# A fused attention and MLP kernel: a table moves engine orders, squares and copies change engine, pairs of transfers become one

## The chip, the cores and the metric

The kernel runs on one core of one Trainium2 chip. The metric is the device time of one execution in microseconds (us), the median of several runs. TensorE is called PE, VectorE DVE, ScalarE ACT, GpSimd POOL and SyncE SP. Transfers are issued from SP, POOL and ACT and are carried out by the core's 16 DMA engines.

## The reference

Cosine attention over 8 batches, 12 heads, 448 tokens and a head size of 64, followed by an MLP over the 3584 tokens whose activation is h·cos(h):

```python
q_n = q / (np.linalg.norm(q, axis=-1, keepdims=True) + 1e-06)
k_n = k / (np.linalg.norm(k, axis=-1, keepdims=True) + 1e-06)
scores = np.matmul(q_n, k_n.transpose(0, 1, 3, 2)) / tau
attn = softmax(scores)                      # tau = 0.1
x = (attn @ v).transpose(0, 2, 1, 3).reshape(3584, 768)
h = x @ w_in                                # 768 x 2048
out = (h * np.cos(h)) @ w_out               # 2048 x 768
```

## The kernel before

**Tiles and stages.** A *quad* is four heads of one batch: three quads to a batch, 24 in all. For each quad q and k are loaded (`Qf`, `Kf`, 448 KB each), squared (`square`), summed over the head size (`add`, DVE), turned into inverse norms (`inverse`: Ln and Exp on ACT, an addition and a reciprocal on DVE), scaled (`scale`) and transposed: by PE and a copy for the first quads (`transpose`), by a transposing DMA later (`turn`). `scores` makes seven pairs of score banks in PSUM, each evacuated by one Exp on ACT into a tile `E` (L556). `attend` multiplies by v.

The softmax's row sums come in two ways. For quads 0 to 5 PE multiplies `E` by ones (`spread`) and ACT inverts the 128-partition result. For quads 6 to 23, in rounds of two quads, `sums` makes a few rows of sums with `sel`, and `invert` takes their Ln and Exp, writes 8 rows of 448 numbers to a scratch tensor `rscr` in DRAM (issued from ACT, L648), and reads them back spread over 64 partitions each into `R` (two buffers; issued from SP, L654, two transfers for each quad, one for each half of the partitions). POOL then multiplies `AVs` by `R` into the MLP's input `xT` (L657).

The MLP works batch by batch: `m1` (96 matmuls of 128x448 a batch, L675, in 8 pairs of PSUM banks; ACT and DVE make h·cos(h) from each pair, L688 to L694), then `m2` over row tiles of 128 tokens (28 tiles, two halves of 384 columns, 16 matmuls each, L703). DVE copies each half to `osb` (three buffers, L711), and SP stores the tile in two transfers of 64 rows (L717).

**What sets the order.** Every operation is recorded by `op` in a `Planner`, which has a duration for each and lays them out per engine. PE's order is the order of recording. Ahead of the first MLP stage the planner is `strict`: ACT, DVE and POOL keep their recorded order as well (`behind`, L50). After that, whichever ready operation has the earliest due time goes first. `VISITS` and `LATER` say, batch by batch, after how many `m2` matmuls PE takes up pieces of the attention of later batches. Waits between engines are put in from the recorded reads and writes. SP, POOL and ACT each issue their transfers in their order, so one that waits holds up those behind it.

**Transfers.** A transfer is described by an access pattern for each side: a list of [step, count] pairs, the outermost first. A store of 64 rows (before) has the patterns [[5376, 64], [1, 768]] in DRAM and [[768, 64], [1, 768]] in SBUF, and a read of `R` has [[0, 64], [1, 896]] and [[896, 64], [1, 896]].

Other lines that are named later: L797 are matmuls without use that keep PE running in the first stretch (`warm`), L399 the loads of q and k, L411 those of v, L421 and L426 those of the two weight matrices (`W1`, `W2`), L524 the copies behind PE's transposes.

Of the kernel before, what the change touches and what calls it, by code (L numbers as in the profile page):

```python
# [9 lines left out]
ALU = mybir.AluOpType  # L10
# [6 lines left out]
class Op:  # L17
    __slots__ = ("i", "eng", "dur", "fn", "reads", "writes", "deps", "dma", "lat", "start", "end",
                 "count", "waits", "known", "prio", "moves", "mode", "chain", "behind", "lead", "packet", "lock")


class Planner:
# [20 lines left out]
    def op(self, eng, dur, fn, r=(), w=(), after=(), dma=None, moves=0, mode="f", chain=None, keep=False, lead=0.0,  # L43
           packet=74, lock=False):
        o = Op()
        o.i, o.eng, o.dur, o.fn, o.dma, o.moves, o.mode, o.chain = (
            len(self.ops), eng, dur, fn, dma, moves, mode, chain)
        o.lat = self.FIRST + moves + self.LAST if dma else self.LAT[eng]
        o.behind, o.lead, o.packet, o.lock = None, lead, packet, lock
        if keep or self.strict and eng in ("act", "dve", "pool"):  # L50
            o.behind, self.tail[eng] = self.tail.get(eng), o
        o.reads, o.writes = tuple(r), tuple(w)
        deps = {a.i for a in after if a is not None}
        for x in o.reads:
            if x in self.last_write:
                deps.add(self.last_write[x].i)
        for x in o.writes:
            if x in self.last_write:
                deps.add(self.last_write[x].i)
            deps.update(p.i for p in self.readers.get(x, ()))  # L60
        deps.discard(o.i)
        o.deps = sorted(deps)
        for x in o.reads:
            self.readers.setdefault(x, []).append(o)
        for x in o.writes:
            self.last_write[x] = o
            self.readers[x] = []
        self.ops.append(o)
        return o
# [12 lines left out]
    PASSES, SPREAD = 0, 1.5  # L82

    def plan(self):

        rng = random.Random(1)
        shift = [0.0] * len(self.ops)
        least = max(o.end for o in self.pass_(shift))
        for _ in range(self.PASSES):
            n = rng.choice((8, 30, 100))  # L90
            i = rng.randrange(len(shift) - n)
            tried = list(shift)
            for k in range(i, i + n):
                tried[k] += rng.gauss(0.0, self.SPREAD)
            end = max(o.end for o in self.pass_(tried))
            if end <= least:
                least, shift = end, tried
        self.order = self.pass_(shift)
        return self.order

    def pass_(self, shift):
# [12 lines left out]
        for o in ops:  # L114
            if o.eng == "pe":
                urge[o.i] = t
                t += o.dur
        later = None
        behind = {}
        for o in reversed(ops):  # L120
            if o.eng == "pe":
                if later is not None:
                    urge[o.i] = min(urge[o.i], urge[later.i] - o.dur)
                later = o
# [10 lines left out]
        pe = [o.i for o in ops if o.eng == "pe"]  # L135
# [139 lines left out]
def bass_cosine_attention__then__act_gcu_kernel(  # L275
# [43 lines left out]
    n2 = ring("n2", 2, [128, 4 * NJ], F32)  # L319
    nrm = ring("nrm", 2, [128, 4 * NJ], F32)  # L320
    rr = ring("rr", 2, [128, 4 * NJ], F32)
    ne = ring("ne", 2, [128, 4 * NJ, 2], F32)
# [39 lines left out]
    for i in range(2):  # L362
        op("dve", 0.1, lambda e, i=i: e.memset(ne[i].ap()[:, :, 1], 1e-6), w=[("eps", i)])
# [67 lines left out]
    def jr(t, w, part, off=0):  # L431
        return bass.AP(t, off + w * H + part[0], [[2 * H, 128], [NJ, 2], [1, part[1] - part[0]]])

    def square(qd, w, eng, part=ALL[0], after=()):
        s, u = qd % 3, qd % 2
        j0, j1 = part
        n = (j1 - j0) / NJ
        f, sq, nm = ((Qf, sqq, "Q"), (Kf, sqk, "K"))[w]
        src = f[s].ap()[:, :, j0:j1]
        dst = sq.ap().rearrange("p (r j) d -> p r j d", r=2)[:, :, j0:j1]  # L440
        if part == ALL[0]:
            src, dst = src.rearrange("p r j d -> p (r j) d"), sq.ap()
        if eng == "act":
            op("act", 0.1 + 0.83 * n, lambda e: e.activation(dst, src, ACT.Square), r=cut(nm + "f", s, part),
               w=cut("sq" + nm, 0, part))
        else:
            op(eng, (1.68 if eng == "pool" else 1.05) * n, lambda e: e.tensor_tensor(dst, src, src, ALU.mult),  # L447
               r=cut(nm + "f", s, part), w=cut("sq" + nm, 0, part), after=after, lock=True)

        def add():  # L450
            return op("dve", 0.07 + 0.95 * n, lambda e: e.tensor_reduce(  # L451
                out=n2[u].ap()[:, H * w:H * w + H] if part == ALL[0] else jr(n2[u], w, part),
                in_=dst, axis=AX.X, op=ALU.add),
                r=cut("sq" + nm, 0, part), w=cut("n2%d" % w, u, part))

        return add

    def inverse(qd, w0, w1, part=ALL[0], after=()):
# [5 lines left out]
        if part == ALL[0]:  # L464
            n = slice(H * w0, H * w1)
            t, z, o = n2[u].ap()[:, n], nrm[u].ap()[:, n], rr[u].ap()[:, n]
        else:
            t, z, o = (jr(a[u], w0, part) for a in (n2, nrm, rr))
# [11 lines left out]
        two_ = ne[u].ap()[:, H * w0:H * w1]  # L480
# [7 lines left out]

    def scale(qd, w, eng="pool", part=ALL[0]):
# [3 lines left out]
        rb = bass.AP(rr[u], w * H + j0, [[2 * H, 128], [NJ, 2], [1, j1 - j0], [0, D]])  # L493
# [16 lines left out]
    def transpose(qd, which, bk, part=ALL[0]):  # L510
# [12 lines left out]
        dst = t[u].ap()[:, j0:j1].rearrange("p j a x -> p (j a x)")  # L523
        op("dve", 0.07 + 0.067 * (j1 - j0), lambda e: e.tensor_copy(dst, src), r=whole(bk),  # L524
# [113 lines left out]
    def invert(quads, bk):  # L638
# [9 lines left out]
        op("act", 0.3, lambda e: e.dma_start(rscr.ap()[8 * n:8 * n + rows, :], Zs[z].ap()[0:32 * np_:16, :]),  # L648
           r=[("Zs", z)], w=[("rs", n)], dma=("rs", z), moves=0.05, lead=LEAD)
        for i, qd in enumerate(quads):  # L650
            u, sl, b = qd % 2, qd % NA, qd // QB
            for r in range(2):
                ap = bass.AP(rscr, (8 * n + 4 * i + 2 * r) * S, [[0, 64], [S, 2], [1, S]])
                op("sp", 0.6, lambda e, r=r, u=u, ap=ap: e.dma_start(R[u].ap()[64 * r:64 * r + 64], ap),  # L654
                   r=[("rs", n)], w=[("R", u, r)], dma=("R", u, r), moves=0.85, packet=140, lead=LEAD)
# [3 lines left out]
                r=[("AV", sl), ("R", u, 0), ("R", u, 1)], w=[("x", b % 2, qd % QB)], lead=LEAD, lock=True)  # L659
# [37 lines left out]
    def m2(t, h, f0, f1, bk):  # L697
# [11 lines left out]
        if f1 == NNB:  # L709
            so = t % 3  # L710
            op("dve", 0.475, lambda e: e.tensor_copy(osb[so].ap()[:, HW * h:HW * h + HW], bank(bk, HW)),  # L711
               r=whole(bk), w=[("o", so, h)])
            if h:
                for sg in range(2):
                    b, cc = divmod(128 * t + 64 * sg, S)
                    dst = bass.AP(out.tensor, (S * b + cc // 64) * KM, [[NJ * KM, 64], [1, KM]])
                    op("sp", 0.6, lambda e, sg=sg, dst=dst: e.dma_start(dst, osb[so].ap()[64 * sg:64 * sg + 64, :]),  # L717
                       r=[("o", so, 0), ("o", so, 1)], w=[("out", t, sg)], dma=("store", so, sg), moves=0.55, packet=121)
# [15 lines left out]
    LATER = {19: 3, 10: -1, 18: -2, 5: 3, 4: 1, 17: 4, 7: -1, 21: -2, 22: -1, 15: -2, 9: 1}  # L734
# [100 lines left out]
    adds[0]()  # L835
# [5 lines left out]
    adds[1]()  # L841
# [19 lines left out]
    addk = square(2, 1, "act")  # L861
# [86 lines left out]
    for c in range(B):  # L948
# [106 lines left out]
```

## Time and profile before

| | |
|---|---|
| median of 3 runs | 425.83 us (425.01 to 428.05) |
| the profiled execution | 424.88 us, of it 423.0 us from the first to the last instruction |
| PE, ACT, DVE, POOL busy | 406.1, 306.3, 269.5, 200.9 us |
| granted PE clock | 1.00 throughout |
| bytes moved | 62.94 MB: 53.87 MB read from HBM, 11.14 MB written |

The batches' `m1` stages begin on PE at 34.4, 89.0, about 148, 195.6, 245.8, 292.9, 346.0 and 379.7 us. The profile's columns are: for a window the span, then each engine's busy time (with its instructions in brackets), the granted clock, the mean busy share of the 16 DMA engines and the GB/s that they moved. In the chain of waits each row has its start, its length and the work that it stands for. In the DMA view a queue's row has its packets, its MB, and the packets' time as a share of 16 engines' span. A row of the issues has the transfer, the queue it is issued from, its count, the size of one, and the median time to landing.

### The profile page before, as it was taken

To read this page: it belongs to the slowest core of one execution; us is meant where nothing else is said; L and a number is where in the kernel's file an instruction comes from. 1 tells how busy PE (TensorE), PEld (TensorE's weight loads), DVE (VectorE), ACT (ScalarE), POOL (GpSimd) and SP (SyncE) were. 2 spreads that over 40 slices of the span, in tenths; PEclk is the share of its full clock that TensorE was granted. 3 is DMA by queue.
4 is the path that set the end of the run, shared out by engine and by line. 5 is a ranking of instruction groups with operands and counts; after the bars stand their busy time and mean duration, and the time that the engine had idled before them with its cause. 6 is when DMAs were issued, how large, how long until landed. Compare 5 with 4: busy or idle time off the path is not lost.

```text
span 423.0 us, 8441 instructions
## 1 busy us (share of the span) xinstructions
PE 406.1 (96%) x3586; PEld 212.6 (50%) x3586; DVE 269.5 (64%) x337; ACT 306.3 (72%) x404; POOL 200.9 (47%) x137
## 2 busy tenths in 40 slices
PE   6879998999999999999999999999999999999995
PEld 5345454445544445445555555445554555555563
DVE  5767886879853659733996269824882228736921
ACT  6998689988888977697787677689678656505700
POOL 3566238792387794758628880559213213000000
PEclk9999999999999999999999999999999999999999
DMA  8999997995099969298909990279805523021022
GB/s 272 259 236 209 242 273 165 186 218 135 4 220 227 283 107 251 67 238 212 229 5 211 206 279 2 52 179 177 166 1 82 128 72 92 2 74 39 0 76 74
DMA packets 68230, 62.94 MB, mean 149 GB/s; under 512 B 39961, under 2 KB 60769, under 8 KB 68193
## 3 DMA queue, kind: packets, MB, share of 16 engines
q1 hardware_dynamic: 57808, 50.48, 48.3%
q0 software_dynamic: 10240, 11.80, 16.8%
q8 instruction: 28, 0.46, 0.5%
q10 hardware_dynamic: 144, 0.13, 0.1%
q14 instruction: 10, 0.07, 0.0%
HBM read 53.87 MB, written 11.14 MB: 154 GB/s over the span
## 4 chain that ended last, share of the span: by engine, by line
PE 77%; DMA 12%; ACT 4%; DVE 3%; POOL 2%; issue 0%; ACTq 0%; SPq 0%
PE PS L703 30%; PE PS L675 30%; PE PS L566 7%; PE PS L549 6%; DMA W<-in_moe_w_out_dram 6%; PE PS L629 3%; DMA Kf<-in_k_dram 3%; ACT E L556 2%; DMA R<-rscr 1%; DVE n L451 1%; PE PS L588 1%; DMA rscr<-Zs 1%; DMA Qf<-in_q_dram 1%; DVE osb L711 1%; POOL xT L657 0%
## 5 line engine op out<-in xcount | busy, mean ns | idle before, releaser
L556 ACT ACTIVATE E<-PS 128x896 bf16<-128x896 f32 x168 | 142.4, 919 | 20.8 <-PE PS L549 18.4
L703 PE MATMUL PS<-W,gT 128*128 128x384 bf16 x896 | 157.0, 327 | 0.0
L675 PE MATMUL PS<-xT,W 128*128 128x448 bf16 x768 | 147.0, 353 | 1.3 <-DVE qT L524 1.0
L703 PEld LDWEIGHTS PS<-W,gT 128*128 128x128 bf16 x896 | 82.9, 98 | 69.8 <-issue 15.9
L675 PEld LDWEIGHTS PS<-xT,W 128*128 128x128 bf16 x768 | 74.7, 98 | 71.7 <-DVE qT L524 1.1
L688 ACT ACTIVATE ar<-PS 128x896 int32<-128x896 f32 x64 | 58.2, 911 | 37.5 <-PE PS L675 37.5
L690 DVE SCALAR_TENSOR_TENSOR ar<-ar,PS 128x896 f32<-128x896 int32 x64 | 69.2, 1083 | 22.3 <-ACT ar L688 22.3
L694 DVE TENSOR_TENSOR gT<-PS,ar 128x896 bf16<-128x896 f32 x64 | 69.5, 1088 | 7.5 <-ACT ar L692 7.1
L692 ACT ACTIVATE ar<-ar 128x896 f32<-128x896 f32 x64 | 60.6, 946 | 18.2 <-DVE ar L690 18.0
L711 DVE COPY osb<-PS 128x384 f32<-128x384 f32 x56 | 31.1, 556 | 61.2 <-PE PS L703 60.5
L657 POOL TENSOR_TENSOR xT<-AVs,R 128x896 bf16<-128x896 f32 x18 | 37.4, 2086 | 49.6 <-DMA R<-rscr 49.6
L549 PE MATMUL PS<-qT,kT 64*64 64x448 bf16 x672 | 49.7, 359 | 5.3 <-ACT E L556 2.8
L447 POOL TENSOR_TENSOR sqq<-Qf 128x896 bf16<-128x896 f32 x22 | 36.9, 1677 | 34.0 <-DVE n L451 14.4
L447 POOL TENSOR_TENSOR sqk<-Kf 128x896 bf16<-128x896 f32 x21 | 36.9, 1756 | 33.2 <-DVE n L451 32.0
L495 POOL TENSOR_TENSOR Qn<-Qf,rr 128x896 bf16<-128x896 f32 x21 | 38.0, 1812 | 24.3 <-DVE rr L487 16.7
L575 DVE COPY AVs<-PS 128x896 f32<-128x896 f32 x21 | 22.8, 1088 | 29.2 <-PE PS L566 29.1
L566 PE MATMUL PS<-E,Vb 64*64 64x448 bf16 x672 | 36.7, 350 | 0.0
L451 DVE TENSOR_REDUCE n<-sqq 128x14 f32<-128x896 bf16 x24 | 25.7, 1072 | 14.3 <-POOL sqq L447 10.2
L549 PEld LDWEIGHTS PS<-qT,kT 64*64 64x64 bf16 x672 | 16.5, 105 | 31.8 <-ACT E L556 12.8
L495 POOL TENSOR_TENSOR Kn<-Kf,rr 128x896 bf16<-128x896 f32 x18 | 30.3, 1685 | 1.8 <-DMA kT<-Kn 1.8
L451 DVE TENSOR_REDUCE n<-sqk 128x14 f32<-128x896 bf16 (+2 forms) x25 | 25.9, 1040 | 5.8 <-POOL sqk L447 5.8
L566 PEld LDWEIGHTS PS<-E,Vb 64*64 64x64 bf16 x672 | 18.8, 107 | 12.7 <-issue 1.9
(45 smaller groups left out, 175.7 us busy)
## 6 DMA issues: line engine op xcount, KB each, us to landing
Qf<-in_q_dram SPq DMA_DIRECT2D x24, 448.0 KB, 5.4
out_dram<-osb SPq DMA_DIRECT2D x56, 192.0 KB, 3.6
Kf<-in_k_dram SPq DMA_DIRECT2D x23, 448.0 KB, 5.9
R<-rscr SPq DMA_DIRECT2D x36, 224.0 KB, 4.5
Vb<-in_v_dram POOLq DMA_DIRECT2D x24, 224.0 KB, 5.7
W<-in_moe_w_in_dram POOLq DMA_DIRECT2D x4, 768.0 KB, 17.7
W<-in_moe_w_out_dram POOLq DMA_DIRECT2D x4, 768.0 KB, 24.4
qT<-Qn SPq DMA_TRANSPOSE x20, 4.1
```

The costliest lines, as they stand in the source:

```text
L447: op(eng, (1.68 if eng == "pool" else 1.05) * n, lambda e: e.tensor_tensor(dst, src, src, ALU.mult), r=cut(nm + "f", s, part), w=cut("sq" ...
L451: return op("dve", 0.07 + 0.95 * n, lambda e: e.tensor_reduce(out=n2[u].ap()[:, H * w:H * w + H] if part == ALL[0] else jr(n2[u], w, part) ...
L495: lambda e: e.tensor_tensor(n[0].ap()[:, j0:j1].rearrange("p j r d -> p r j d"), f[s].ap()[:, :, j0:j1], rb, ALU.mult),
L549: ins = e.matmul(bank(bs + r, S, 64 * a, 64 * a + 64), kT[u].ap()[64 * r:64 * r + 64, j, a, :], qT[u].ap()[64 * r:64 * r + 64, :, a, :], s ...
L556: act("exp", 0.81, lambda e: e.activation(E[es].ap(), two(bs), ACT.Exp, bias=0.0, scale=INV_TAU), r=pair(bs), w=[("E", es)], chain="E")
L566: ins = e.matmul(bank(bk + a, S, 64 * r, 64 * r + 64), Vb[vs].ap()[64 * a:64 * a + 64, r, j, :], E[es].ap()[64 * a:64 * a + 64, r, :], sta ...
L675: ins = e.matmul(bank(bk + i2), W1.ap()[:, i, 128 * nb:128 * nb + 128], xT[c % 2].ap()[:, i, :], start=(i == 0), stop=(i == NKC - 1))
L688: op("act", 0.815, lambda e: e.activation(ar[s].ap().bitcast(I32), two(bk), ACT.Identity, bias=0.25, scale=INV2PI), r=bs, w=[("ar", s)])
L690: op("dve", 1.005, lambda e: e.scalar_tensor_tensor(ar[s].ap(), ar[s].ap().bitcast(I32), -2.0 * math.pi, two(bk), ALU.mult, ALU.add), r=bs ...
L692: act("sin", 0.86, lambda e: e.activation(ar[s].ap(), ar[s].ap(), ACT.Sin, bias=GUARD * math.pi / 2.0, scale=GUARD), r=[("ar", s)], w=[("a ...
L694: op("dve", 1.01, lambda e: e.tensor_tensor(gT.ap()[:, 2 * pr:2 * pr + 2, col:col + S], two(bk), ar[s].ap(), ALU.mult), r=bs + [("ar", s)] ...
L703: ins = e.matmul(bank(bk, HW), gT.ap()[:, f, col:col + 128], W2.ap()[:, f, HW * h:HW * h + HW], start=(f == 0), stop=(f == NNB - 1))
```

## The change

The changed parts are given cut to their core. What is issued, and in which order, was read from the built programs.

A table `MOVE` (118 entries; number of the recorded operation, shift) reorders the strict stretch ahead of the first MLP stage, PE's order too; the unused search (`PASSES`) goes.

```diff
+        o.key = o.i + (self.MOVE.get(o.i, 0) if self.strict else 0)
         if keep or self.strict and eng in ("act", "dve", "pool"):
-            o.behind, self.tail[eng] = self.tail.get(eng), o
+            self.tail.setdefault(eng, []).append(o)
...
+    MOVE = {18: 22.0, 105: 4.0, 22: -33.0, 101: -10.5, 123: -0.5, 200: 24.0, 120: -11.0, 69: -12.0, 191: -11.0,
...
     def plan(self):
+        for line in self.tail.values():
+            line.sort(key=lambda o: o.key)
+            for a, b in zip(line, line[1:]):
+                b.behind = a
+        self.order = self.pass_([0.0] * len(self.ops))
...
+        pe = [o.i for o in sorted((o for o in ops if o.eng == "pe"), key=lambda o: o.key)]
```

In that stretch the built orders differ as follows. On ACT the square of quad 2's k is gone (it is on POOL) and the exponentials behind it move up. On POOL quad 2's two squares stand between the loads of `W2`, the first of which is issued right behind those of `W1`, and the load of quad 3's v comes after the four loads of `W2`, not before. On PE some warm-up matmuls, score and row-sum groups change places by one to three groups. DVE's sums of squares change places with copies next to them.

```diff
-    addk = square(2, 1, "act")
+    addk = square(2, 1, "pool")
```

The second of these lines stands ahead of the norms of quad 1, the first stood further down, behind the scores of group 6.

The norms' small tensors (`n2`, `nrm`, `rr`, `ne`) become one tensor each with an index for the parity of the quad, and a function that takes the norms of two quads at once is added. Nothing in the changed file calls it: the built orders still have an Ln, an Exp, an addition and a reciprocal for quad 3 and for quad 4.

```diff
+    def inverse_two():
+        flat = "p u n -> p (u n)"
+        t, z, o = (a.ap().rearrange(flat) for a in (n2, nrm, rr))
...
+        act("exp", 0.17, lambda e: e.activation(z, t, ACT.Ln, bias=1e-30, scale=1.0), r=c2, w=x)
...
+        op("dve", 0.55, lambda e: e.reciprocal(o, z), r=x, w=y)
```

The two copies behind PE's transposes of quad 3, in the middle of the first `m1` stage, go from DVE to ACT:

```diff
-                    transpose(FIRST, w, at_bank[pr] + w)
+                    transpose(FIRST, w, at_bank[pr] + w, eng="act")
```

The read of a quad's inverse sums becomes one transfer (36 become 18), and so does the store of a tile where its 128 rows lie in one batch. Of the 28 tiles 23 become one whole transfer, four that cross a batch's end keep two, and the last is stored in two halves of 384 columns, each as soon as it is copied (56 transfers become 33):

```diff
-            for r in range(2):
-                ap = bass.AP(rscr, (8 * n + 4 * i + 2 * r) * S, [[0, 64], [S, 2], [1, S]])
-                op("sp", 0.6, lambda e, r=r, u=u, ap=ap: e.dma_start(R[u].ap()[64 * r:64 * r + 64], ap),
-                   r=[("rs", n)], w=[("R", u, r)], dma=("R", u, r), moves=0.85, packet=140, lead=LEAD)
+            ap = bass.AP(rscr, (8 * n + 4 * i) * S, [[2 * S, 2], [0, 64], [S, 2], [1, S]])
+            op("sp", 0.6, lambda e, u=u, ap=ap: e.dma_start(R[u].ap(), ap),
+               r=[("rs", n)], w=[("R", u)], dma=("R", u), moves=1.9, packet=140, lead=LEAD)
...
+    def store(t, x0, x1, parts):
+        so = t % 3
+        b, cc = divmod(128 * t, S)
+        n = 2 if cc + 64 < S else 1
+        for sg in range(0, 2, n):
+            b, cc = divmod(128 * t + 64 * sg, S)
+            dst = bass.AP(out.tensor, (S * b + cc // 64) * KM + x0, [[KM, n], [NJ * KM, 64], [1, x1 - x0]])
+            src = osb[so].ap()[64 * sg:64 * (sg + n), x0:x1]
+            op("sp", 0.6, lambda e, dst=dst, src=src: e.dma_start(dst, src), r=parts, w=[("out", t, sg, x0)],
+               dma=("store", so, x0, sg), moves=0.55 * n * (x1 - x0) / KM, packet=121)
```

In the built program the patterns of these transfers are [[896, 2], [0, 64], [1, 896]] in DRAM and [[896, 128], [1, 1], [1, 896]] in SBUF for `R`, and [[768, 2], [5376, 64], [1, 768]] in DRAM and [[768, 128], [1, 1], [1, 768]] in SBUF for a tile.

The entries of `VISITS` move by up to five matmuls, `LATER` has other entries, and the planner is told other durations for the writes to `rscr`.

More of the change, by code (lines that the diff above doesn't have):

```diff
@@ L18 @@
     __slots__ = ("i", "eng", "dur", "fn", "reads", "writes", "deps", "dma", "lat", "start", "end",
-                 "count", "waits", "known", "prio", "moves", "mode", "chain", "behind", "lead", "packet", "lock")
+                 "count", "waits", "known", "prio", "moves", "mode", "chain", "behind", "lead", "packet", "lock", "key")
 class Planner:
@@ L80, in land @@
         return s + took + self.LAST
-    PASSES, SPREAD = 0, 1.5
-    def plan(self):
[L86 to L98, printed above, removed]
+    MOVE = {18: 22.0, 105: 4.0, 22: -33.0, 101: -10.5, 123: -0.5, 200: 24.0, 120: -11.0, 69: -12.0, 191: -11.0,
[11 rows of a table added]
+    def plan(self):
+        for line in self.tail.values():
[3 more added lines that the diff above has]
+        self.order = self.pass_([0.0] * len(self.ops))
         return self.order
@@ L113, in pass_ @@
         t, urge = 0.0, [1e9] * len(ops)
[L114 to L118, printed above, removed]
+        pe = [o.i for o in sorted((o for o in ops if o.eng == "pe"), key=lambda o: o.key)]
+        for i in pe:
+            urge[i] = t
+            t += ops[i].dur
+        later = dict(zip(pe, pe[1:]))
         behind = {}
         for o in reversed(ops):
[L121 to L124, printed above, removed]
+            if o.i in later:
+                urge[o.i] = min(urge[o.i], urge[later[o.i]] - o.dur)
             if o.chain:
@@ L318, in bass_cosine_attention__then__act_gcu_kernel @@
     sqk = sb("sqk", [128, 2 * NJ, D], BF16)
[L319 to L322, printed above, removed]
+    n2 = sb("n2", [128, 2, 4 * NJ], F32)
+    nrm = sb("nrm", [128, 2, 4 * NJ], F32)
+    rr = sb("rr", [128, 2, 4 * NJ], F32)
+    ne = sb("ne", [128, 2, 4 * NJ, 2], F32)
     Qn = ring("Qn", 1, [128, NJ, 2, D], BF16)
@@ L429, in bass_cosine_attention__then__act_gcu_kernel, with jr @@
     H, NLEAD = 2 * NJ, 5.0
-    def jr(t, w, part, off=0):
-        return bass.AP(t, off + w * H + part[0], [[2 * H, 128], [NJ, 2], [1, part[1] - part[0]]])
+    def jr(t, u, w, part):
+        return bass.AP(t, (2 * u + w) * H + part[0], [[4 * H, 128], [NJ, 2], [1, part[1] - part[0]]])
     def square(qd, w, eng, part=ALL[0], after=()):
@@ L451, in add @@
             return op("dve", 0.07 + 0.95 * n, lambda e: e.tensor_reduce(
-                out=n2[u].ap()[:, H * w:H * w + H] if part == ALL[0] else jr(n2[u], w, part),
+                out=n2.ap()[:, u, H * w:H * w + H] if part == ALL[0] else jr(n2, u, w, part),
                 in_=dst, axis=AX.X, op=ALU.add),
@@ L465, in inverse @@
             n = slice(H * w0, H * w1)
-            t, z, o = n2[u].ap()[:, n], nrm[u].ap()[:, n], rr[u].ap()[:, n]
+            t, z, o = n2.ap()[:, u, n], nrm.ap()[:, u, n], rr.ap()[:, u, n]
         else:
-            t, z, o = (jr(a[u], w0, part) for a in (n2, nrm, rr))
+            t, z, o = (jr(a, u, w0, part) for a in (n2, nrm, rr))
         act("exp", 0.12, lambda e: e.activation(z, t, ACT.Ln, bias=1e-30, scale=1.0),
@@ L487, in inverse @@
         op("dve", 0.3, lambda e: e.reciprocal(o, z), r=x, w=y, lead=lead)
+    def inverse_two():
+        flat = "p u n -> p (u n)"
+        t, z, o = (a.ap().rearrange(flat) for a in (n2, nrm, rr))
+        c2, x, y = ([c for u in range(2) for w in range(2) for c in cut("%s%d" % (k, w), u, ALL[0])] for k in ("n2", "nrm", "rr"))
+        both = ne.ap().rearrange("p u n i -> p (u n) i")
+        act("exp", 0.17, lambda e: e.activation(z, t, ACT.Ln, bias=1e-30, scale=1.0), r=c2, w=x)
+        act("exp", 0.17, lambda e: e.activation(both[:, :, 0], z, ACT.Exp, bias=0.0, scale=0.5), r=x,
+            w=[("ne", 0), ("ne", 1)])
+        op("dve", 0.2, lambda e: e.tensor_reduce(out=z, in_=both, axis=AX.X, op=ALU.add),
+           r=[(k, u) for k in ("ne", "eps") for u in range(2)], w=x)
+        op("dve", 0.55, lambda e: e.reciprocal(o, z), r=x, w=y)
     def scale(qd, w, eng="pool", part=ALL[0]):
@@ L508, in norm_b, with transpose @@
         return last
-    def transpose(qd, which, bk, part=ALL[0]):
+    def transpose(qd, which, bk, part=ALL[0], eng="dve"):
         u = qd % 3
@@ L523, in transpose @@
         dst = t[u].ap()[:, j0:j1].rearrange("p j a x -> p (j a x)")
+        if eng == "act":
+            op("act", 0.13 + 0.067 * (j1 - j0), lambda e: e.activation(dst, src, ACT.Copy), r=whole(bk), w=cut(nm + "T", u, part))
+            return
         op("dve", 0.07 + 0.067 * (j1 - j0), lambda e: e.tensor_copy(dst, src), r=whole(bk),
@@ L647, in invert @@
         act("exp", 0.47, lambda e: e.activation(zz, zz, ACT.Exp, bias=0.0, scale=-1.0), r=[("Zs", z)], w=[("Zs", z)], lead=LEAD)
[L648 to L649 removed]
+        op("act", 0.57, lambda e: e.dma_start(rscr.ap()[8 * n:8 * n + rows, :], Zs[z].ap()[0:32 * np_:16, :]),
+           r=[("Zs", z)], w=[("rs", n)], dma=("rs", z), moves=0.6, lead=LEAD)
         for i, qd in enumerate(quads):
             u, sl, b = qd % 2, qd % NA, qd // QB
[L652 to L655 removed]
+            ap = bass.AP(rscr, (8 * n + 4 * i) * S, [[2 * S, 2], [0, 64], [S, 2], [1, S]])
+            op("sp", 0.6, lambda e, u=u, ap=ap: e.dma_start(R[u].ap(), ap),
+               r=[("rs", n)], w=[("R", u)], dma=("R", u), moves=1.9, packet=140, lead=LEAD)
             c0 = 2 * (qd % QB)
@@ L710, in m2 @@
             so = t % 3
+            end = t == B * S // 128 - 1
             op("dve", 0.475, lambda e: e.tensor_copy(osb[so].ap()[:, HW * h:HW * h + HW], bank(bk, HW)),
                r=whole(bk), w=[("o", so, h)])
[L713 to L718, printed above, removed]
+            if end:
+                store(t, HW * h, HW * h + HW, [("o", so, h)])
+            elif h:
+                store(t, 0, KM, [("o", so, 0), ("o", so, 1)])
+    def store(t, x0, x1, parts):
[8 more added lines that the diff above has]
+               dma=("store", so, x0, sg), moves=0.55 * n * (x1 - x0) / KM, packet=121)
     QUADS = [4, 5, 3, 3, 3, 3, 0, 0]
@@ L733, in bass_cosine_attention__then__act_gcu_kernel @@
     ]
-    LATER = {19: 3, 10: -1, 18: -2, 5: 3, 4: 1, 17: 4, 7: -1, 21: -2, 22: -1, 15: -2, 9: 1}
+    LATER = {19: 3, 18: -2, 5: 3, 7: -2, 21: -2, 15: 4, 9: 3, 10: -1, 23: 1, 12: -1}
     E1, E2 = NNB - 6, NNB - 4
@@ L834, in bass_cosine_attention__then__act_gcu_kernel @@
     adds = [square(1, w, "act") for w in range(2)]
-    adds[0]()
+    adds[1]()
     load_qk(3)
```

11 lines of the change are left out of this document (5 added, 6 removed), and 25 rows, old and new, of tables (MOVE, VISITS).

## The prediction

> **What bounds the kernel now.** I read first the page's totals and its chain of waits:
>
> ```profile
> PE 406.1 (96%) x3586; PEld 212.6 (50%) x3586; DVE 269.5 (64%) x337; ACT 306.3 (72%) x404; POOL 200.9 (47%) x137
> ...
> PE 77%; DMA 12%; ACT 4%; DVE 3%; POOL 2%; issue 0%; ACTq 0%; SPq 0%
> ```
>
> Of the span of 423.0 us PE idles 16.9. I asked next where, in five windows, and for two short ones in which nearly all traffic is of one kind (reads of `R` in 350 to 353; a tile's store and nothing else in 376 to 379):
>
> ```profile
> core 0: us, PE busy (x) PEld busy (x) DVE busy (x) ACT busy (x) POOL busy (x), PEclk, DMA share, GB/s
> 0.00:34.00 34.00, 25.47 (x392) 15.82 (x396) 23.15 (x42) 29.36 (x50) 18.48 (x24) 1.00 1.05 252
> 34.00:63.00 29.00, 28.04 (x188) 14.53 (x181) 23.89 (x29) 22.22 (x29) 11.26 (x8) 1.00 1.16 243
> 63.00:127.00 64.00, 62.08 (x626) 31.05 (x625) 49.62 (x61) 57.55 (x78) 44.26 (x27) 1.00 0.74 156
> 127.00:350.00 223.00, 221.77 (x1999) 112.83 (x1997) 132.20 (x161) 169.80 (x219) 122.77 (x78) 1.00 0.66 152
> 350.00:423.00 73.00, 68.75 (x395) 38.33 (x393) 40.60 (x46) 27.40 (x31) 4.15 (x2) 1.00 0.19 48
> ...
> 350.00:353.00 3.00, 3.00 (x18) 1.54 (x17) 1.98 (x3) 1.94 (x3) 0.61 (x1) 1.00 0.97 239
> 376.00:379.00 3.00, 3.00 (x20) 1.84 (x19) 0.56 (x1) 0.00 (x0) 0.00 (x0) 1.00 0.51 131
> ```
>
> PE's idle time is 8.5 us up to 34, 1.0 to 63, 1.9 to 127, 1.2 in the long middle, 4.3 in the last window (4.2 of it after the last matmul). So reordering can win little behind 34, and all of its idle time together is 4%. The 16 DMA engines are full to 63 us and two thirds busy in the middle. Then the DMA view, for the bytes and packets:
>
> ```profile
> q1 hardware_dynamic: 57808, 50.48, 48.3%
> q0 software_dynamic: 10240, 11.80, 16.8%
> ...
> q10 hardware_dynamic: 144, 0.13, 0.1%
> ...
> R<-rscr SPq DMA_DIRECT2D x36, 224.0 KB, 4.5
> ...
> rscr<-Zs ACTq DMA_DIRECT2D x9, 14.0 KB
> ```
>
> The packet counts tell over how many engines a transfer is spread. POOL's queue q0 has 32 transfers with 9728 rows of data, so 512 packets over, 16 for each: one closing packet (4 bytes in the packet records) per engine. ACT's q10 has nine transfers of 8 rows, 72 of data, and 72 over: 8 each. The one kind of transfer whose outermost count is under 16 (8) ran on 8 engines. All others have 64 or 128 outermost on both sides. Last, the place where the sums' way is on the chain:
>
> ```profile
> 137.05 4.43 DMA rscr<-Zs
> 141.50 0.48 SPq L654
> 142.01 5.41 DMA R<-rscr
> 147.49 2.09 POOL xT L657
> ```
>
> At this turn to the third batch's `m1` (PE's next row in the chain, at 149.63) the read of `R` has no slack.
>
> **The change, part by part.** Sums are against the profiled 424.9 us (423.0 and 1.9 around it); the median is 0.9 above it.
>
> *Square of quad 2's k to POOL.* ACT loses one Square of 0.94 us (17.67 in its timeline). From 11.2 to 34 ACT idles only 0.2 us, and its last exponential ahead of `m1` ends at 33.75, so `m1` starts 0.94 earlier. POOL's 1.68 us go into its 4.79 us of idle time before 17.48.
>
> *The table.* With ACT full from 11.2 on, the order can add at most those 0.2 us and PE's waits on it, and can lose one such wait (0.4 to 0.8 each). Moving `W2`'s issues forward brings no byte earlier, since the engines are full to 63; the loads of quads 3 and 4 behind them are covered by POOL's wait for DVE (1.96 us at 25.5). Quad 3's v is first used after 63. Without that cover a wait of 1 to 2 us comes. I take -0.1, bounds -0.5 to +2.
>
> *Norms of quads 3 and 4 in one.* Not issued: 0.
>
> *Two copies to ACT.* PE waits 0.96 us at 43.1 for DVE's second copy, which ends at 43.60. ACT is free from its L688 at 42.34; the nearest row for its copy is L556 (919 ns for as many elements; DVE's takes 0.61), so the pair ends at 44.2, and two L692 behind them come 1.8 us later. I take +0.4, bounds -1.0 to +1.8.
>
> *`VISITS`, `LATER`.* PE's whole idle time from 63 to 350 is 3.2 us, the bound of the gain; one missed turn costs 0.4 to 0.8. I take -0.3.
>
> *Fewer issues.* 18 and 23 issues of about 0.6 us leave SP's queue, which has 0% of the chain; at 141.50 half a microsecond is on it: -0.5. At the end one store's issue and its 0.6 us less after the last copy: -0.9 if the transfers keep 16 engines.
>
> So far -1.0 - 0.1 + 0.4 - 0.3 - 0.5 - 0.9 = -2.4: 422.5.
>
> *The joined transfers.* Their DRAM pattern now has 2 outermost. By the q10 row, where outermost 8 meant 8 engines, I take it that they run on 2 engines. The page "DMA: Bandwidth & Descriptors" of the Trainium skill (section "Why a DMA increments its semaphore by 16 and not by 1") states it as a rule: the number of engines is the largest up to 16 that divides the slowest count other than 1 of both patterns, which makes 2 of 2 and 128. The q10 row agrees with it (8 and 8), though 8 rows could not have used more engines under any rule.
>
> Price: in the two short windows an engine moved 239/(0.97 x 16) = 15.4 GB/s of `R` and 131/(0.51 x 16) = 16.1 of stores. A quad's 458,752 bytes on two engines then take 14.9 us, a tile's 393,216 bytes 12.2. The other bound are the fastest tenth of the packet records: 140 ns for 3584 bytes of `R`, 121 for 3072 of a store, so 64 rows an engine take 9.0 and 7.7. Fourteen engines fewer pull at the same memory, so I lean to the fast bound.
>
> Now the middle, 127 to 350, where all 18 reads of `R` lie. An engine's work there is 0.66 x 223 = 147 us. `R` is 8.26 MB of it (33.5 us at 15.4 GB/s), 34 stores 6.69 MB (26 us), so 88 is other traffic, a sixteenth of which stays on each of the two engines. Of the 17 tiles stored there 15 become joined. Work for each of the two engines:
> - fast: 18 x 9.0 + 15 x 7.7 + 88 + 3 (the two split tiles) = 368 us
> - slow: 18 x 14.9 + 15 x 12.2 + 91 = 542 us
>
> against a stretch of 223. It must grow by 145 to 319. SP's queue is in order, so loads and transposes behind a read of `R` have their two sixteenths served after it, and PE waits. After 350 six joined tiles take 46 to 73 us beside 73 of PE work and hide; the last half tile lands 3 to 4 us later than in the sum above. That gives 422.5 + 148 = 570 to 422.5 + 323 = 745. The two queues will not be full at every turn, since SP also waits for DVE and POOL with only two `R` and three `osb`: a tenth of the 277 us of `R` and stores, 28 us, on top of the fast bound. **600 us.**
>
> **Rivals.**
>
> *A: the joined transfers keep 16 engines.* For it: q10's 8 may just be its 8 rows, and a pattern may be split where 128 rows are there. Against: no row of the trace shows a spread over any but the outermost count. Time 422.5; the bounds above give 418 to 428. The mechanism decides at one point, the number of closing packets of a store. The same page ("Rules for kernel authors") advises one transfer over 128 partitions in place of two over halves, which speaks for the change; by it the time is this rival's.
>
> *B: two engines, but fast enough for the work.* In windows with a share of 1.16 the packets' times overlap, so an engine may do more than its packets' times say. If it does 2.1 times as much as in the fast bound, (162 + 116)/2.1 + 91 = 223 fits the stretch, and only the landing is late: two reads take 8.5 us and some 3 us of latency (4.5 to landing now, less 1.8 of moving) against 6 now, 5 later. The slack is nothing at 148 and about 5 us at the next turn (`R` asked for at 180, `xT` about 190, needed at 195.6). One to five such turns give 428 to 448. Against: an overlap of 1.16 alone gives (162 + 116)/1.16 + 91 = 331, still 108 over the stretch, 530.
>
> *C: the loads in the first stretch collide in the new order* and cost 2 us: inside A's range, no case of its own.
>
> **How the numbers follow.** Two engines bind: 0.60, with its own range of 530 to 745. B 0.08. A 0.32; 1% of the median, 4.3 us, is about what a measurement can tell, and A's 422.5 lies 3.3 under the median, so of A 0.12 is faster, 0.165 the same, 0.035 slower. Together slower 0.715, same 0.165, faster 0.12. The range must reach down to A to leave out no more than 2 in 10: 416 to 745.
>
> **What would show it.** On q1 there were 54,272 rows of data and 3,536 = 16 x 221 closing packets (transposes have two sets). The last tile, stored by halves, makes 128 rows more. Right, if q1 has 2,278 closing packets, 56,678 in all (2 for each of 43 joined transfers), reads of `R` land 10 to 30 us after their issue, the DMA share's mean falls with the longer span, and the chain is of `R` and `osb` transfers with PE waiting for L657. For the small steps: `m1` starts near 33.4, and PE's wait at 43 is 0.9 to 1.5. Wrong, if q1 has 2,880 closing packets, 57,280 in all, and `R` lands in 4 to 6 us: then A holds, and the time is the sum of the small steps.

## The result, and the profile after

| | before | after |
|---|---|---|
| median, side by side on one chip (6 runs each) | 426.91 us | 587.25 us (585.32 to 591.35) |
| ratio | | 1.3776 [1.3709, 1.3842] |
| profiled execution, its span | 424.88, 423.0 us | 589.33, 587.2 us |
| PE busy, PE idle | 406.1, 16.9 us | 439.4, 147.8 us |

The change makes the kernel slower by 38%. The forecast was 600 us on the ground that the joined transfers run on two DMA engines. The page of the changed kernel, its totals, its chain of waits and its rows on queues and issues:

```profile
PE 439.4 (75%) x3586; PEld 221.4 (38%) x3586; DVE 268.0 (46%) x335; ACT 309.5 (53%) x405; POOL 201.7 (34%) x138
...
q1 hardware_dynamic: 56678, 50.47, 49.6%
q0 software_dynamic: 10240, 11.80, 12.6%
...
DMA 44%; PE 21%; POOL 13%; issue 11%; ACT 4%; DVE 3%; SPq 1%; POOLq 0%
...
out_dram<-osb SPq DMA_DIRECT2D x23, 384.0 KB
R<-rscr SPq DMA_DIRECT2D x18, 448.0 KB
```

Packets first: 56,678 on q1, of which 54,400 are rows of data, so 2,278 closing ones: two for each of the 43 joined transfers and sixteen for each of the others (a transpose has two such sets). The times in the packet records say the same: between the first and the last row of `R`, 386 us, rows of `R` or of a store are in flight two at a time for 262 us; before, when there were any, it was most often sixteen at a time (19.7 us). The chain is no longer PE's (77% before, 21% now) but the transfers'. The two joined kinds have no landing time in this view, as the writes to `rscr` (8 engines) had none before; the kinds on 16 engines have one. DVE, ACT and POOL are as busy as before. PE is busy for 33 us longer with the same 3586 matmuls, and idle for 131 us longer.

The waits of the changed kernel (us in all, times, longest):

```profile
POOL xT L672 <- DMA R<-rscr: 203.3, 18, 22.8
PE PS L690 <- POOL xT L672: 50.5, 8, 11.8
PE PS L565 <- DMA kT<-Kn: 27.0, 4, 19.9
DVE n L451 <- POOL sqq L447: 88.0, 9, 21.0
```

POOL waits for every one of the 18 reads (before: 49.6 us, 11 times, at most 14.0), and PE then waits for POOL. The third row is the other way in which the reads hurt: a transposed k that lies behind them. The fourth row is a third way: POOL works in order, so the squares of a later quad stand behind the `xT` that waits, DVE's sums wait for these squares, and PE waits for what DVE does behind the sums (at 311.5, for instance, 17.1 us for a copy to `AVs`). Two rows of POOL's timeline show what one read costs. Both reads of this round were issued from 141.79 on; the last number is POOL's wait.

```profile
153.80 2.07 POOL L672 TENSOR_TENSOR xT<-AVs,R 128x896 bf16<-128x896 f32 x1 [8.82 <-DMA R<-rscr]
163.25 2.07 POOL L672 TENSOR_TENSOR xT<-AVs,R 128x896 bf16<-128x896 f32 x1 [7.37 <-DMA R<-rscr]
```

Both starts are set by a landing, and the second is 9.4 us after the first: that is the time of one `R` on two engines (9.0 in the next round), at the forecast's fast bound of 9.0 and not at the slow one of 14.9. The reads land 12 to 31 us after their issue. SP's timeline from the same moment, with the length of each group of issues:

```profile
141.79 1.16 SPq L669 DMA_DIRECT2D R<-rscr  x2
143.00 6.16 SPq L399 DMA_DIRECT2D Kf<-in_k_dram  x1
149.20 0.54 SPq L742 DMA_DIRECT2D out_dram<-osb  x1
149.85 17.80 SPq L547 DMA_TRANSPOSE qT<-Qn  x1
```

Behind the reads even the issuing stands still: 17.80 us for one transposing transfer, whose issue took 1.2 to 3.7 us before. And the windows:

```profile
core 0: us, PE busy (x) PEld busy (x) DVE busy (x) ACT busy (x) POOL busy (x), PEclk, DMA share, GB/s
...
63.00:127.00 64.00, 54.80 (x508) 27.12 (x508) 43.68 (x53) 48.34 (x64) 32.08 (x20) 0.95 0.84 127
127.00:350.00 223.00, 152.07 (x1261) 72.62 (x1260) 82.62 (x106) 109.43 (x146) 93.20 (x60) 0.83 0.70 107
```

In the long middle PE gets through 1261 matmuls where it got through 1999, at a granted clock of 0.83. The DMA share of 0.70 looks like that of before (0.66), but 107 GB/s moved in place of 152. The share counts a packet's whole time, and the transposes' packets of 256 bytes took 76 ns in the mean, where it was 28. The share alone would have shown nothing.

### The profile page after: what moved, and what is told of

It reads as the page before. It is cut to its first block, busy times and chain, and to the rows that moved or that the text cites. A ratio compares the mean times of both kernels' runs of the same rounds, so it can differ in the third digit from the quotient of the medians.

```text
span 587.2 us, 8388 instructions
## 1 busy us (share of the span) xinstructions
PE 439.4 (75%) x3586; PEld 221.4 (38%) x3586; DVE 268.0 (46%) x335; ACT 309.5 (53%) x405; POOL 201.7 (34%) x138
## 3 DMA queue, kind: packets, MB, share of 16 engines
q1 hardware_dynamic: 56678, 50.47, 49.6%
## 4 chain that ended last, share of the span: by engine, by line
DMA 44%; PE 21%; POOL 13%; issue 11%; ACT 4%; DVE 3%; SPq 1%; POOLq 0%
DMA R<-rscr 23%; DMA qT<-Qn 11%; PE PS L718 8%; PE PS L690 8%; DMA rscr<-Zs 5%; POOL xT L672 3%; POOL sqq L447 3%; DMA Qf<-in_q_dram 3%; POOL Qn L508 2%; POOL Kn L508 2%; PE PS L582 2%; ACT E L572 2%; PE PS L565 2%; POOL sqk L447 2%; DMA kT<-Kn 1%
## 5 line engine op out<-in xcount | busy, mean ns | idle before, releaser
L690 PE MATMUL PS<-xT,W 128*128 128x448 bf16 x768 | 165.9, 380 | 69.1 <-POOL xT L672 50.5
L572 ACT ACTIVATE E<-PS 128x896 bf16<-128x896 f32 x168 | 144.1, 917 | 52.5 <-PE PS L565 49.2
L718 PE MATMUL PS<-W,gT 128*128 128x384 bf16 x896 | 160.0, 331 | 0.2 <-DVE osb L727 0.2
L690 PEld LDWEIGHTS PS<-xT,W 128*128 128x128 bf16 x768 | 78.2, 104 | 155.1 <-POOL xT L672 42.6
L672 POOL TENSOR_TENSOR xT<-AVs,R 128x896 bf16<-128x896 f32 x18 | 37.3, 2074 | 203.3 <-DMA R<-rscr 203.3
L565 PE MATMUL PS<-qT,kT 64*64 64x448 bf16 x672 | 52.4, 375 | 56.9 <-DMA kT<-Kn 27.0
L565 PEld LDWEIGHTS PS<-qT,kT 64*64 64x64 bf16 x672 | 17.1, 108 | 84.9 <-issue 42.5
L582 PE MATMUL PS<-E,Vb 64*64 64x448 bf16 x672 | 41.2, 379 | 0.1
L582 PEld LDWEIGHTS PS<-E,Vb 64*64 64x64 bf16 x672 | 20.0, 114 | 15.6 <-issue 5.3
```

Source lines behind the costliest of these rows:

```text
L565: ins = e.matmul(bank(bs + r, S, 64 * a, 64 * a + 64), kT[u].ap()[64 * r:64 * r + 64, j, a, :], qT[u].ap()[64 * r:64 * r + 64, :, a, :], s ...
L572: act("exp", 0.81, lambda e: e.activation(E[es].ap(), two(bs), ACT.Exp, bias=0.0, scale=INV_TAU), r=pair(bs), w=[("E", es)], chain="E")
L582: ins = e.matmul(bank(bk + a, S, 64 * r, 64 * r + 64), Vb[vs].ap()[64 * a:64 * a + 64, r, j, :], E[es].ap()[64 * a:64 * a + 64, r, :], sta ...
L672: op("pool", 2.04, lambda e, u=u, sl=sl, b=b, c0=c0: e.tensor_tensor(xT[b % 2].ap()[:, c0:c0 + 2, :], AVs[sl].ap(), R[u].ap(), ALU.mult), ...
L690: ins = e.matmul(bank(bk + i2), W1.ap()[:, i, 128 * nb:128 * nb + 128], xT[c % 2].ap()[:, i, :], start=(i == 0), stop=(i == NKC - 1))
L718: ins = e.matmul(bank(bk, HW), gT.ap()[:, f, col:col + 128], W2.ap()[:, f, HW * h:HW * h + HW], start=(f == 0), stop=(f == NNB - 1))
```

## The experiments

The theory: the transfers that are joined have 2 as their outermost count, run on two engines, and these two become the bound of the middle stretch. Its rivals: joining as such costs the time (one long transfer and one wait in place of two), whatever the engines; only one of the two kinds matters; or the new orders do it. "Split" below means as before: two transfers of 64 rows each.

**One kind split, both split, and the joined transfers alone.** The edit of e1 (`R` split in the changed kernel), of e2 (tiles split; the last tile still goes in two halves of columns), e3 is both, and e4 is the kernel before with only the joined transfers:

```diff
-            ap = bass.AP(rscr, (8 * n + 4 * i) * S, [[2 * S, 2], [0, 64], [S, 2], [1, S]])
-            op("sp", 0.6, lambda e, u=u, ap=ap: e.dma_start(R[u].ap(), ap),
+            for r in range(2):
+                ap = bass.AP(rscr, (8 * n + 4 * i + 2 * r) * S, [[0, 64], [S, 2], [1, S]])
+                op("sp", 0.6, lambda e, r=r, u=u, ap=ap: e.dma_start(R[u].ap()[64 * r:64 * r + 64], ap),
...
-        n = 2 if cc + 64 < S else 1
+        n = 1
```

> The changed kernel with the reads of R in two transfers of 64 rows again; the stores stay joined. Two engines bind: R goes back to 16 engines (36 issues, q1 has 18 x 32 - 18 x 2 = 540 more closing packets, 2,818), the two engines keep the stores, so of the 161 us lost about 18 x 7.7 = 140 us of work leaves the two engines: 430 to 480 us. Rival A is out. Rival 'the stores are what costs': still over 550.

> The changed kernel with every tile's store in two transfers of 64 rows again; the reads of R stay joined. If reads of R on two engines are most of the cost, as the chain of the changed kernel has it (R 23% of the span, stores 0%): 500 to 570 us. If the two engines are bound by the sum of both kinds, R and stores count about alike per byte (8.3 and 9.4 MB): near the time of the run with R split, 450 to 500.

> The changed kernel with both kinds in two transfers again; the table, the squares on POOL, the copies on ACT, the new visits and the last tile in halves stay. Two engines as the whole cause of the slowdown: 418 to 428, with 422.5 by the sum of the small steps. If the table or the copies cost more than a few us (m1 began at 36.7 in the changed kernel, 34.4 before): over 428.

> The kernel before with nothing but the joined transfers. Two engines as the whole cause: within 15 us of the changed kernel, 570 to 605. If the other edits make it worse: nearer to the kernel before, under 550.

Measured (kernel before in the same job: 425.9, 17 runs): e1 484.63 and e2 499.54 (one run each), e3 **428.88** (427.17 to 431.48, 12 runs, ratio 1.0065 [1.0039, 1.0091]), e4 **574.14** (one run). The new orders are thus not the cause: with all of them in place and the transfers split, 1.0065 is left, and the joined transfers alone make 574 of the old kernel. Neither is it one kind only; e1 came out a little over its range, e2 at the border between those of its two theories, e3 0.9 us over the range it had for two engines as the whole cause, and e4 within its own, 13 us under the changed kernel. Where each costs is read from SP's timeline: the issue of the first read of `R`, of the last ones, and the span's end cut each run in three (us, worked out from these rows):

| | up to the first `R` | from there to the last ones | from there to the end |
|---|---|---|---|
| before | 127.3 | 220.5 | 75.2 |
| e3, none joined | 127.9 | 225.4 | 74.8 |
| e1, tiles joined | 137.5 | 260.3 | 85.0 |
| e2, `R` joined | 128.7 | 296.7 | 72.0 |
| after, both | 141.8 | 347.9 | 97.5 |

Joined tiles cost 9.6 us ahead of the first `R`, 35 in the middle and 10 at the end; joined reads cost 71, all in the middle. Alone the two make 55 and 69 us of span, together 159: more than their sum. A queue that has reserves left until the second load comes would do that; the runs do not show whether this is the reason.

**The same transfers, another outermost count.** e5 has the tiles split and `R` in two transfers for each quad, same bytes, same number, same destination. Only the pattern that repeats a row for 64 partitions is written differently: 64 (e3), 16 x 4, 4 x 16 or 2 x 32.

```diff
-                ap = bass.AP(rscr, (8 * n + 4 * i + 2 * r) * S, [[0, 64], [S, 2], [1, S]])
+                ap = bass.AP(rscr, (8 * n + 4 * i + 2 * r) * S, [[0, 2], [0, 32], [S, 2], [1, S]])
```

> As e3 (both kinds in two transfers), but each 64-row read of R has its pattern written as [[0, 2], [0, 32], [1, 896]]: the same rows, bytes and number of transfers, only the outermost count is 2. The outermost count sets the engines: q1 has 36 x 14 = 504 closing packets fewer than e3 (57,464), and the time is about that of e2, where a joined read had 2 outermost: 485 to 515. Rival, that it is the joining (longer transfers, fewer issues): as e3, 428.

> The same with [[0, 4], [0, 16], [1, 896]]. Outermost count 4 means 4 engines: 36 x 12 = 432 closing packets fewer than e3 (57,536). A quad's two halves are 2 x 16 x 0.14 = 4.5 us on each of four engines, so a round's last R lands some 7 us later than e3's and the turns of the batches lose up to that: 432 to 460. Rival: 428.

> The control: [[0, 16], [0, 4], [1, 896]], three dimensions as in the other two, 16 outermost. 16 engines, q1 as in e3 (57,968), 426 to 432. If the split pattern itself costs (not the engines), it is slower than e3 here too.

Measured, one run each: **500.74** with 2, **450.42** with 4, **432.25** with 16, beside 428.88 with 64. The pages of the three, q1 and the reads, in this order:

```profile
q1 hardware_dynamic: 57464, 50.47, 49.7%
...
R<-rscr SPq DMA_DIRECT2D x36, 224.0 KB
```

```profile
q1 hardware_dynamic: 57536, 50.48, 50.9%
...
R<-rscr SPq DMA_DIRECT2D x36, 224.0 KB
```

```profile
q1 hardware_dynamic: 57968, 50.48, 46.8%
...
R<-rscr SPq DMA_DIRECT2D x36, 224.0 KB, 4.5
```

From e3's 57,968 the first is 504 = 36 x 14 packets lower and the second 432 = 36 x 12; the third is equal. Each transfer has 2, 4 or 16 closing packets, rows in flight stand most often two, four or sixteen at a time in the packet records, and the landing time is back with 16. That refutes joining as the cause for the reads: with two transfers a quad and a count of 2 the time is e2's (500.7 and 499.5). The times fell in the ranges expected, the control's 0.25 us over. For the tiles the count was not varied in this way; there e1 shows two engines by its packets (57,218 on q1, so 2,818 closing ones, as expected), and a loss of 56 us against e3. The Trainium skill's page "DMA: Bandwidth & Descriptors" (section "Why a DMA increments its semaphore by 16 and not by 1") has the number of engines as the largest up to 16 that divides both patterns' slowest counts; these three packet counts agree with it.

The run with 4 says more. Its wait for the reads:

```profile
POOL xT L673 <- DMA R<-rscr: 86.7, 17, 17.2
```

A row took 171 ns in its packet records, so the reads put 18 x 32 x 0.171 = 98 us on each of the four engines, and with the forecast's 88 and 26 of other work that is an estimate of 212. The stretch was 220 us before and took 247 here, so the four engines were not full all the time, and the kernel still loses 21.5 us: POOL waits for 17 of the 18 reads. That fits the second rival's mechanism, late landings without full engines; no run shows it apart from the load, which is close to the 220. With 2 the same sum is 114 + 18 x 64 x 0.153 = 290, and the stretch took 299.

**What the orders cost.** e3 is 3 us above the kernel before, where the small steps were to save 2.4. Its PE timeline at the start of the first `m1`, and its wait at the third batch's:

```profile
35.38 6.98 PE L691 MATMUL PS<-xT,W 128*128 128x448 bf16 x36 [1.52 <-DMA W<-in_moe_w_in_dram]
...
153.17 2.17 PE L691 MATMUL PS<-xT,W 128*128 128x448 bf16 x7 [3.06 <-POOL xT L673]
```

PE is ready at 33.86, earlier than before (34.40), and waits 1.52 us for `W1`. Tile names alone did not show why; the patterns in the built program do: the table's first entry puts one of the four loads of `W1`, partitions 64 to 127 of the columns that are used first, behind the other three. e7 is e3 without this entry, e8 also has the old `VISITS` and `LATER`, e9 also the old engine for quad 3's copies:

```diff
-    MOVE = {18: 22.0, 105: 4.0, 22: -33.0, 101: -10.5, 123: -0.5, 200: 24.0, 120: -11.0, 69: -12.0, 191: -11.0,
+    MOVE = {105: 4.0, 22: -33.0, 101: -10.5, 123: -0.5, 200: 24.0, 120: -11.0, 69: -12.0, 191: -11.0,
...
-                    transpose(FIRST, w, at_bank[pr] + w, eng="act")
+                    transpose(FIRST, w, at_bank[pr] + w)
```

> As e3, without the table's entry for operation 18, which moves the load of the second half of W1's first columns behind the other three loads of W1. If the wait of 1.5 us ahead of the first m1 is for that load: the wait is gone, m1 begins at 33.9, the time is 1 to 2 us under e3's 428.9 (426.9 to 427.9). If the loads of W2 that are issued earlier take the bandwidth: m1 still begins at 35 or later, no change.

> As e7 (both kinds in two transfers, W1's loads in the recorded order), with VISITS and LATER of the kernel before. In e7 PE still waits 1.5 us at the turn to the third batch for R, which is asked for later than in the kernel before; if the moved visits cost that, the wait goes to under 0.5 and the time is 1 to 2 us under e7's 426.1: 424 to 425. If they are neutral: 425.5 to 426.5.

> As e8, with the two copies of quad 3 on DVE again. PE waited 0.96 us there with DVE's copies and 0.6 to 1.0 with ACT's, so by PE's wait alone no more than 0.4 either way; if the two later L708 on ACT hold up later pairs, up to 1 us faster than e8.

Measured, 11 or 12 runs each: e7 **426.06** (ratio 1.0014 [0.9981, 1.0047]), e8 **429.52** (1.0057 [1.0023, 1.009]), e9 **428.27** (1.0048 [1.0019, 1.0078]). By the medians the entry costs 2.8 us, more than the 1 to 2 expected (the two ratios' intervals just overlap), and in e7's trace its wait is gone; the wait for `xT` is down to 1.5 us as well. The old `VISITS` did take the wait for `xT` away, and yet e8 is slower: my expectation for it fell. Its waits and POOL's order around the place:

```profile
PE PS L565 <- DMA kT<-Kn: 2.5, 1, 2.5
```

```profile
130.15 2.08 POOL L673 TENSOR_TENSOR xT<-AVs,R 128x896 bf16<-128x896 f32 x1 [0.60 <-DMA R<-rscr]
133.27 2.10 POOL L673 TENSOR_TENSOR xT<-AVs,R 128x896 bf16<-128x896 f32 x1 [1.05 <-DMA R<-rscr]
135.33 1.69 POOL L508 TENSOR_TENSOR Qn<-Qf,rr 128x896 bf16<-128x896 f32 x1
136.97 1.69 POOL L508 TENSOR_TENSOR Kn<-Kf,rr 128x896 bf16<-128x896 f32 x1
```

POOL makes both `xT` first and then a quad's `Qn` and `Kn`; the transposing transfer of that `Kn` is issued at 138.69 and PE needs `kT` at 139.16. Among the edits left, the one that bears on this place is the planner's durations for the writes to `rscr`, which now lie near what they take (0.57 and 0.6, before 0.3 and 0.05). So I asked for the old ones, in e9 (making e10) and in e7 (making e11):

```diff
-        op("act", 0.57, lambda e: e.dma_start(rscr.ap()[8 * n:8 * n + rows, :], Zs[z].ap()[0:32 * np_:16, :]),
-           r=[("Zs", z)], w=[("rs", n)], dma=("rs", z), moves=0.6, lead=LEAD)
+        op("act", 0.3, lambda e: e.dma_start(rscr.ap()[8 * n:8 * n + rows, :], Zs[z].ap()[0:32 * np_:16, :]),
+           r=[("Zs", z)], w=[("rs", n)], dma=("rs", z), moves=0.05, lead=LEAD)
```

> As e9, with the planner's old durations for the writes to rscr, so that SP's order behind the first MLP stage is nearly that of the kernel before. Left of the change: the table without its entry 18, quad 2's k squared on POOL, the last tile in halves. If e9's wait of 2.3 us for a transpose at 148 comes from the new durations: it goes, and the first stretch's gain shows, 423.5 to 425.5 (the first m1 at 33.4 to 33.9, the last store 0.5 earlier). If the table itself is worth nothing: 426, as before.

> As e7, with the planner's old durations for the writes to rscr: new visits, copies on ACT. If the new visits suit the new durations: slower than e7, 427 to 430, with a wait at 148. If the durations do not matter: as e7, 425.5 to 426.5.

Measured, 12 runs each: e10 **424.27** (422.65 to 425.85, ratio **0.9945 [0.9916, 0.9975]**), e11 425.57 (1.0003 [0.9968, 1.0038]). POOL's order in e10 at the same place:

```profile
128.48 1.69 POOL L508 TENSOR_TENSOR Qn<-Qf,rr 128x896 bf16<-128x896 f32 x1 [0.57 <-DMA qT<-Qn]
130.13 1.69 POOL L508 TENSOR_TENSOR Kn<-Kf,rr 128x896 bf16<-128x896 f32 x1
133.66 4.15 POOL L673 TENSOR_TENSOR xT<-AVs,R 128x896 bf16<-128x896 f32 x2 [1.84 <-DMA R<-rscr]
```

`Qn` and `Kn` now use the time in which the reads are under way, the transpose is issued at 132.80, and PE's wait for `kT` is gone. So durations nearer the truth cost 4 us with the old `VISITS` (e9 against e10) and nothing that shows with the new ones (e7 against e11, 0.5 us with intervals that overlap): the old `VISITS` go with the old durations, the new ones do about as well with either. e10 beats both kernels. What it keeps of the change is the table without its first entry, the square on POOL (with quad 1's two sums in the other order), the merged small tensors and the last tile in two halves. Which of these gives the gain was not separated. The halves are seen in the trace: from the end of the last copy to the end of the span it is 3.2 us, 3.7 before. A gain ahead of the first `m1` is not: it began at 35.77 in e10's profiled execution, where 33.4 to 33.9 was expected (that execution took 425.85, the longest of the twelve).

What stays open: e8's executions run from 425.91 to 430.79, and the profiled one took 426.27, so its 2.5 us of waiting need not be all that the slower ones lose. A joined transfer with 16 or more outermost on both sides, for which the partitions would have to hold the rows in another order, wasn't tried.

## Why the prediction was right

The steps, by their own numbers:

- *Two engines.* 2,278 closing packets forecast, 2,278 counted. The sign and the size hang on this step, and e5 shows it for the reads with nothing else changed. The first rival (16 engines, 422.5) fell with it. The time alone would have said little, since the range of 416 to 745 held this rival too; the packets decide. The Trainium skill's advice on the same page (section "Rules for kernel authors") to use one transfer over 128 partitions in place of two over halves speaks for the change; here it gave 574.14 in place of 425.9, since the joined pattern's DRAM side begins with 2. Another row of that section of the Trainium skill warns of just that, an outermost count under 16.
- *The price of one.* Forecast 9.0 to 14.9 us for a read of `R`, leaning to the fast bound: 9.0 and 9.4 measured. A row of `R` took 147 ns in the mean (226 before), one of a tile 141 (171 before). The e5 runs have the same rows on 2, 4 and 16 engines at 153, 171 and 208 ns, so the argument held that fewer engines at work make each of them faster, and the fastest tenth of the packets of before was a good guide.
- *The stretch with the reads.* Forecast 368 us (+145) for the fast bound and 28 more of idle time, 396 in all; from the first row of `R` to the last it was 386 (225 before, 229 in e3). So this part was 10 us too long. How long the two engines were idle is not shown, since the packet records do not name the engine: rows of `R` or of a store are in flight for 293 of the 386 us, and the 93 that are left are near the 88 that the forecast had for other traffic.
- *The chain.* Expected of `R` and `osb` transfers. `R` is on it (23% of the span), with POOL's L672 behind it as forecast; a store is nowhere on it up to the last copy. The tiles cost their time by holding up other transfers: in e1, with the tiles alone joined, POOL waits 24.6 us for transposed q (3.4 before) and 24.7 for loads of q (12.8 before), and no store is on the chain there either.
- *Terms that were left out.* The sum had nothing for the joined tiles ahead of the first `R` and only 3 us behind the last copy. Both were there. Up to the first `R` the table shows 13.9 us more than in e3; 9.6 of it are the tiles' (e1; e4 has 9.5 over the kernel before), and 1.4 of the rest are the later first `m1` (36.74 against 35.38). At the end the last tiles queue up on two engines. DVE's timeline has the last copy and SP's the last issues:

```profile
570.84 0.56 DVE L727 COPY osb<-PS 128x384 f32<-128x384 f32 x1 [2.04 <-PE PS L718]
```

```profile
515.85 59.76 SPq L742 DMA_DIRECT2D out_dram<-osb  x9
```

  The copy ends at 571.4 and the span at 587.2: 15.8 us, where it was 3.7. In the last batch a tile is done every 5.2 us and its rows take 7.6 to 8.8 on two engines, so six tiles do not hide beside PE's work, as the forecast had it for all but the last half. And yet the time from the last row of `R` to the end is shorter than in e3, 58 us and not 69, since less of PE's work is left by then (216 matmuls, 375 in e3). So against e3 the forecast missed 14 us ahead of the reads and had 16 too many in the middle and 14 too many behind. Part of this cancels, which is luck: the change costs 158.4 us, where 177.5 was forecast from 422.5.
- *The small steps.* Forecast -2.4; e3 shows +3.0. The table was given -0.1 with a bound of +2: its first entry costs 2.8, by the wrong load of `W1` last, a collision in the first stretch of the kind the third rival had, with another place. Without the wait for `W1` PE is ready for the first `m1` at 33.40 to 33.48 in six executions (e1, e2, e5 with 2 and with 4, e8, e11) and at 33.86 and 33.99 in e3 and e5 with 16, where it began at 34.40 before and at 34.24 in e4: about the 0.94 forecast, though the square and the table were not taken apart. It is later (34.40 to 36.74) in e7, e9, e10 and the changed kernel, whose granted clock was 0.66 to 0.83 from 10 to 20 us (1.00 before); in the changed kernel the last part of quad 0's k also landed 1.9 us later than before. PE's wait of 0.96 at 43.1 was misread: it is for the first copy, which ends at 43.07, and not for the second at 43.60. The copies on ACT cost PE a wait of 1.04 in e3 (0.9 to 1.5 forecast) and make no difference that shows (e8 against e9). `VISITS` was priced at one missed turn of 0.4 to 0.8; the missed turn of e3 is 3.06. Behind the last copy 0.9 was to be saved with 16 engines; e3 saves 0.5.
- *The second rival* (engines fast enough, landings late) had the wrong price here, but fits what happens with four engines.

## What to carry to other kernels

Before two transfers are joined, write down the outermost count of both sides of the new pattern: in these runs a leading 2, be it a repeat (e5) or a step to the next rows (the joined reads and tiles), put the whole transfer on two engines, and later transfers on that queue paid. In a profile, count the closing packets per transfer and look for issue rows without a landing time; the DMA share did not show it. An order that was found for one set of planner durations can lose its worth with another: the old `VISITS` lost 4 us with the new durations (e9 against e10), the new ones nothing that shows. e10, with the old pair and the table without its first entry, is 0.55% faster than the kernel before.

## What the runs showed of the hardware

- A transfer on two engines also holds up transfers on sixteen: the transposes' 256-byte packets took 76 ns in the mean and 11.3 us at most (28 ns and 1.8 us before), and the issue of one took up to 17.80 us of SP's time.
- The granted clock was lower in the stretches where PE waited long, so that these waits cost twice: the same 3586 matmuls keep PE busy for 33 of the changed kernel's 164 us of longer span, at a clock of 0.83 in the middle (1.00 before). In e3 the single wait of 3.06 us is followed by 0.83 in the ten microseconds from 150 to 160; in e8 the clock stayed at 1.00 after a wait of 2.54 us. Long single waits are not the only case: in e7, e9 and e10 it was 0.83 from 10 to 20 us, with no wait over 1.1 us between the matmuls up to there.
- The loss is not in proportion to one over the engines: from e3 it is 71.9 us with 2, 21.5 with 4 and 3.4 with 16 (one run each; e3's own runs reach 2.6 above their median).
